# Loads on two rings in turn, alpha ahead of its unit, and a bf16 cast before the transposes, in a gated linear attention with adapters

## The chip, the cores and the metric

The kernel runs on one core of one Trainium2 chip. The metric is the device time of one execution in microseconds (us); lower is better. A core has five engines with an instruction stream each: TensorE (PE; its weight loads are shown as PEld), VectorE (DVE), ScalarE (ACT), GpSimd (POOL) and SyncE (SP). Each stream runs in order. SP and ACT can issue DMA transfers, each into a ring of its own; both rings are worked off by the same 16 DMA engines.

## What is computed

Four batches of eight heads go through a linear attention with a decay for each channel, and its output, 3072 rows of 384, through a mixture of eight low-rank adapters of which each row takes its two best:

```python
# q, k, v, alpha: (4, 8, 768, 48), f32
for t in range(S):
    state = alpha[:, :, t, :, None] * state + np.einsum('bhd,bhe->bhde', k[:, :, t], v[:, :, t])
    y[:, :, t] = np.einsum('bhd,bhde->bhe', q[:, :, t], state)
x = y.transpose(0, 2, 1, 3).reshape(B * S, H * D)      # 3072 x 384
logits = x @ w_gate                                    # 8 experts
# the two best per row, softmax over them -> w
out = x + sum(w[e] * (x @ A[e]) @ B[e] for the two e)  # A: 384 x 16, B: 16 x 384
```

## The kernel before

**Units.** The sequence is cut into chunks of 128 steps. A unit is one chunk of one batch, all eight heads: 6 chunks x 4 batches = 24 units, numbered 0 to 23. Each needs four loads of 192 KB, a chunk of alpha (a), k, q and v. In DRAM a row of a head is 48 floats, so the loads consist of pieces of 192 bytes. The loads go into two sets of buffers, one for even and one for odd batches; a load for unit u overwrites what unit u-12 read.

**Stages of a unit**, by the names that the planner uses, with the engine and the line of the operation:

- `ln` (ACT, L374): logarithm of alpha, for two units at once except for units 0 and 1.
- `cum` (PE, L379 to L385): cumulative sums of the logarithms, by matmuls with triangular matrices. `exp` (ACT, L390): their exponentials.
- `kg` (POOL, L395): k and q times these factors, to bf16. `vb` (POOL, L403): v cast to bf16.
- `tr` (PE, L409): eight transposes of kg's result. `kq` (ACT, L413): copy out of PSUM.
- `at` (PE, L421): the scores. `msk` (DVE, L426): times the causal mask.
- `st` (DVE, L433) and `kv` (PE, L441 to L446): the state from unit to unit within a batch. `av` (PE, L456 to L463): the output of the unit.
- `ysb` (ACT, L468): that output to SBUF in f32. `xt` (PE, L481): three transposes of it, in f32. `xs` (ACT, L486): copy to SBUF as bf16.
- For a group of one to three units: `z` (PE, L500) multiplies by the gate and all A; `gm`, `df`, `ge`, `gx`, `wu`, `dn`, `w` (DVE, and ACT's L524) find the two best and their weights; `zw` (DVE, L549), `zt` (PE, L558), `zs` (ACT, L564).
- For each unit `dl` (PE, L569) multiplies by B and `o` (DVE, L577) adds x. `store` (SP, L600) writes the unit's 192 KB.

**Order.** When the program is built, a list scheduler (`_order`) plays all stages with a duration for each, buffer counts (`KEEP`), PSUM slots (`SLOTS`), priorities (`PRIO`, a figure per stage, plus `PERIOD` per unit) and assumed arrival times of the loads (`_arrivals`). The order in which it starts the stages is the order in which they are emitted, and thereby the order of each engine's stream. Nothing is reordered at run time.

**Loads.** `_plan` lists them as a, k, q, v of unit 0, then of unit 1, and so on. `_ring` gives the first six to SP and ACT in turn; after them every fourth, which is v, goes to ACT and the other three to SP. On ACT a load is an entry of the planner (`ld`) and stands in ACT's stream between its activations, some 5 us (`LEAD`) before the load's assumed arrival. SP has no other work than loads and, after the last load, the stores; `pump` emits SP's loads by the planner's clock. The adapters' weights are three loads on SP (`load_weights`, L297), emitted when 20 loads are out, and three casts on DVE (`cast_weights`, L339), emitted before the first `xs`. Transfers share eight semaphores in rotation, so an issue also waits until the transfer that used its semaphore before has landed.

Of the kernel before, what the change touches and what calls it, by code (L numbers as in the profile page):

```python
# [30 lines left out]
GROUPS = [[0, 1, 2], [3, 4, 5], [6, 7, 8], [9, 10, 11], [12, 13, 14], [15, 16, 17],  # L31
          [18, 19, 20], [21, 22], [23]]
LNS = [[0], [1]] + [[u, u + 1] for u in range(2, NU, 2)]
CAST = set()
LEAD = 5.
FIRST = 6


def _ring(i, item):
    return "ACT" if (i % 2 if i < FIRST else i % 4 == 3) else "SP"  # L40

def _act(n):
# [15 lines left out]
def _pe(t):  # L62
# [3 lines left out]
SMALL = (.2, .09)  # L66
KEEP = dict(lg=2, ex=3, kg=4, kt=4, am=3, sb=2, vb=4, xs=9)
SLOTS = dict(C=1, A=1, M=3)
PRIO = dict(ln=-27.4, cum=-33.5, exp=14.2, kg=-6.0, vb=0.6, tr=4.7, kq=-8.2, at=6.7, msk=15.1,
            st=25.4, kv=6.9, av=-15.0, ysb=22.1, xb=5.9, xt=12.5, xs=-29.2, z=13.2, gm=32.7,  # L70
            df=16.8, ge=17.3, gx=21.3, wu=-9.0, dn=-22.2, w=39.9, zw=20.3, zt=1.9, zs=21.7,
            dl=6.9, o=21.2)
PERIOD = 2.0
SLACK = 0


def _plan():
    plan = []
    for u in range(NU):
        b, c = divmod(u, NCH)  # L80
        plan += [(x, b, c) for x in "akqv"]
    return plan


def _arrivals(plan):
    t, arr = 2.6, {}
    for i, (x, b, c) in enumerate(plan):
        t += 4.2 if c is None else .75
        for j in (range(NCH) if c is None else (c,)):
            arr[x, b * NCH + j] = t  # L90
        arr["due", i] = t - LEAD
    return arr


def _ops(arr):
    ops = {}

    def add(name, eng, length, deps, war=(), alloc=None, frees=None):
        ops[name] = (eng, length, list(deps), list(war), alloc, frees)

    gof = {u: g for g, us in enumerate(GROUPS) for u in us}
    lof = {u: us for us in LNS for u in us}
    prev = []
    for i, (x, b, c) in enumerate(_plan()):
        if i >= FIRST and _ring(i, (x, b, c)) == "ACT":
            war = []
            for j in (range(NCH) if c is None else (c,)):
                u = (b - 2) * NCH + j
                if u >= 0:
                    war.append(dict(a=("ln", lof[u][0]), k=("kg", u), q=("kg", u), v=("vb", u))[x])  # L110
            add(("ld", i), "ACT", (.5, .45), [("due", i)], war + prev)
            prev = [("ld", i)]
    for i, us in enumerate(LNS):
        war = [("cum", u) for u in LNS[i - KEEP["lg"]]] if i >= KEEP["lg"] else []
        add(("ln", us[0]), "ACT", _act(DM * len(us) + 30), [("a", u) for u in us], war)
    for u in range(NU):
        c = u % NCH
        p = u - KEEP["ex"]
        add(("cum", u), "PE", _pe(.49), [("ln", lof[u][0])], alloc="C")
        add(("exp", u), "ACT", _act(776), [("cum", u)],  # L120
            [("kg", p)] + ([("st", p)] if p % NCH else []), frees=("cum", u))
        p = u - KEEP["kg"]
        add(("kg", u), "POOL", _gp(768), [("exp", u), ("k", u), ("q", u)],
            [("tr", p)] + ([("kv", p)] if p % NCH < NCH - 1 else []))
        add(("vb", u), "POOL", _gpc(DM), [("v", u)], [("av", u - KEEP["vb"])])
        add(("tr", u), "PE", _pe(.48), [("kg", u)], alloc="M")
        add(("kq", u), "ACT", _act(512), [("tr", u)], [("av", u - KEEP["kt"])], frees=("tr", u))
        add(("at", u), "PE", _pe(.40), [("kq", u)], alloc="A")
        add(("msk", u), "DVE", _dve(1024), [("at", u)], [("av", u - KEEP["am"])], frees=("at", u))
        if c:  # L130
            add(("st", u), "DVE", _dve(DM), [("kv", u - 1), ("exp", u)], [("av", u - KEEP["sb"])])
        if c < NCH - 1:
            add(("kv", u), "PE", _pe(.33 if c else .17),
                [("vb", u), ("kg", u)] + ([("st", u)] if c else []),
                [] if c or not u else [("st", u - 1)])
        add(("av", u), "PE", _pe(.49 if c else .32),
            [("msk", u), ("vb", u), ("kq", u)] + ([("st", u)] if c else []), alloc="M")
        add(("ysb", u), "ACT", _act(DM), [("av", u)], frees=("av", u))
        if u in CAST:
            add(("xb", u), "POOL", _gpc(DM), [("ysb", u)])  # L140
            add(("xt", u), "PE", _pe(.17), [("xb", u)], alloc="M")
        else:
            add(("xt", u), "PE", _pe(.38), [("ysb", u)], alloc="M")
        p = u - KEEP["xs"]
        add(("xs", u), "ACT", _act(DM), [("xt", u)], [("z", gof[p])] if p >= 0 else [],
            frees=("xt", u))
    for g, us in enumerate(GROUPS):
        n = len(us)
        add(("z", g), "PE", _pe(.18 * n), [("xs", u) for u in us], alloc="M")
        add(("gm", g), "DVE", (.17 + .13 * (n - 1), .13 * n), [("z", g)])  # L150
        add(("df", g), "DVE", SMALL, [("gm", g)])
        add(("ge", g), "DVE", SMALL, [("gm", g)])
        add(("gx", g), "ACT", _act(E * n), [("df", g)])
        add(("wu", g), "DVE", SMALL, [("gx", g), ("ge", g)])
        add(("dn", g), "DVE", SMALL, [("wu", g)])
        add(("w", g), "DVE", (.4, .29), [("dn", g)])
        add(("zw", g), "DVE", _dve(P * n), [("w", g)], frees=("z", g))
        add(("zt", g), "PE", _pe(.057 * n), [("zw", g)], alloc="M")
        add(("zs", g), "ACT", _act(64 * n), [("zt", g)], frees=("zt", g))
        for u in us:  # L160
            add(("dl", u), "PE", _pe(.165), [("zs", g)], alloc="M")
            add(("o", u), "DVE", _dve(DM), [("dl", u)], frees=("dl", u))
    return ops
# [76 lines left out]
def kernel(  # L240
# [21 lines left out]
    ats = ctx.enter_context(tc.tile_pool(name="ats", bufs=KEEP["am"]))  # L262
    sbs = ctx.enter_context(tc.tile_pool(name="sbs", bufs=KEEP["sb"]))
    xss = ctx.enter_context(tc.tile_pool(name="xss", bufs=KEEP["xs"]))
    gate = ctx.enter_context(tc.tile_pool(name="gate", bufs=2))
    ps = ctx.enter_context(tc.tile_pool(name="ps", bufs=1, space=bass.MemoryType.PSUM))

# [13 lines left out]
    def view(t):  # L281
        return t.rearrange("p (h c) d -> p c h d", h=H)[:, :, :, 0:D]

    def load(item, eng):
        x, b, c = item
        t, src = home(x, b), SRC[x][b]
        if c is None:
            eng.dma_start(out=t[:, :, 0:D], in_=src.rearrange("h (c j) d -> j (h c) d", j=C))
        else:
            eng.dma_start(out=view(t)[:, c],  # L290
                          in_=src[:, c * C:(c + 1) * C, :].rearrange("h j d -> j h d"))

    W_st = consts.tile([P, E, NF, R], F4, name="W_st")
    G_st = consts.tile([P, NF, E], F4, name="G_st")
    B_st = consts.tile([P, DM], F4, name="B_st")

    def load_weights():  # L297
        nc.sync.dma_start(out=W_st.rearrange("p e i r -> p e (i r)"),  # L298
                          in_=moe_A.rearrange("e (p i) r -> p e (i r)", i=NF))
        nc.sync.dma_start(out=G_st, in_=moe_w_gate.rearrange("(p i) e -> p i e", i=NF))  # L300
        nc.sync.dma_start(out=B_st, in_=moe_B.rearrange("e r f -> (e r) f"))

    queue = list(enumerate(plan))
    for i in range(FIRST):
        load(queue.pop(0)[1], nc.sync if _ring(i, plan[i]) == "SP" else nc.scalar)
    rings = {r: [x for x in queue if _ring(*x) == r] for r in ("SP", "ACT")}

    suf = consts.tile([P, P], F2, name="suf")
    nc.gpsimd.memset(suf, 1.0)
# [260 lines left out]
                         start=True, stop=True)  # L570

    def ld(i):
        assert rings["ACT"][0][0] == i
        load(rings["ACT"].pop(0)[1], nc.scalar)

    def o(u):
        nc.vector.tensor_tensor(out=o_t[u], in0=bank("dl", u)[:, 0:DM], in1=o_t[u], op=ALU.add)  # L577
# [3 lines left out]
               w=w, zw=zw, zt=zt, zs=zs, dl=dl, o=o)  # L581
    READ = dict(a="ln", k="kg", q="kg", v="vb")
    reads = defaultdict(set)
    weights = 20
    done = []

    def pump(now):
        q = rings["SP"]
        while q:
            i, (x, b, c) = q[0]  # L590
            if arr["due", i] > now or any(
                    (b - 2) * NCH + j not in reads[x]
                    for j in (range(NCH) if c is None else (c,)) if b > 1):
                return
            load(q.pop(0)[1], nc.sync)

    def store(u):
        b, c = divmod(u, NCH)
# [2 lines left out]

    with tc.manual_schedule():
        for s, i in order:
            if (s, i) == ("xs", 0):
                cast_weights()
            RUN[s](i)
            for x, r in READ.items():
                if r == s:
                    for u in (LNS[lof[i][0]] if s == "ln" else (i,)):
                        reads[x].add(u)  # L610
            pump(when[s, i][0])
            if weights and len(plan) - len(rings["SP"]) - len(rings["ACT"]) >= weights:
                load_weights()
                weights = None
            if s == "o":
                done.append(i)
            if not rings["SP"] and not rings["ACT"]:
                while done:
                    store(done.pop(0))

# [29 lines left out]
```

## Time and profile before

| | us |
|---|---|
| median of 3 runs | 113.31 (113.3 to 113.52) |
| the profiled execution | 113.9 |
| its span, first to last instruction | 112.2 |

| engine | busy us | share of the span |
|---|---|---|
| PE | 80.6 | 72% |
| DVE | 69.1 | 62% |
| ACT | 66.2 | 59% |
| POOL | 56.2 | 50% |

The span is what the profile's rows cover; some time of an execution lies outside it. Busy time of PE is modelled at its ends, so a busy PE need not be PE at its peak. The page also has HBM reads of 19.28 MB and writes of 4.72 MB, and per line the operations that this text needs: L395 (kg) takes 1818 ns, L403 (vb) 509, L426 (msk) 1221, L390 (exp) 822, L413 (kq) 584, L468 (ysb) 483, L486 (xs) 480, and L481 (the f32 transposes) 315 a piece against 238 for the bf16 ones of L409. Landing of a load takes 4.0 to 4.5 us from its issue at the median.

How to read the views: the chain of waits follows the work that ended last back to what released it, so its shares say what the end of the execution hung on. The view of waits sums, for each operation, the time its engine stood idle before it, by what ended the wait. The windows cut the span into stretches and give busy time, the granted clock of PE (1.00 is full) and the rate of the DMA engines in each. SPq and ACTq are the issues of DMAs by SP and ACT.

### The profile page before, as it was taken

How to read it: one execution, taken by the hardware profiler on the slowest of the kernel's cores; microseconds unless marked ns; L12 is line 12 of the kernel's file. 1: busy time of each engine (PE TensorE's matmuls, PEld its weight loads, DVE VectorE, ACT ScalarE, POOL GpSimd, SP SyncE). 2: the span in 40 equal slices, each digit the busy share in tenths (PEclk: the TensorE clock that was granted, in tenths of full speed). 3: DMA queues.
4: the chain of work that ended last, by engine and by line, in shares of the span. 5: the costliest groups of instructions: out<-in, count | busy, mean ns of one | idle time of the engine just before them, and what ended most of it. 6: DMA issues, size and time to landing. Idle time of an engine off the chain costs nothing.

```text
span 112.2 us, 2916 instructions
## 1 busy us (share of the span) xinstructions
PE 80.6 (72%) x1112; PEld 62.2 (55%) x1112; DVE 69.1 (62%) x170; ACT 66.2 (59%) x128; POOL 56.2 (50%) x58
## 2 busy tenths in 40 slices
PE   0346994099995496978947969899395699996540
PEld 0124863067874286856836748579283478974210
DVE  4004330765595287899575396967289265998990
ACT  4244476046973767967818769696592745754310
POOL 5077418605949278492691676839287076000000
PEclk9999999558999999999997699999999656999975
DMA  2999999899999899999989999999899999013064
GB/s 57 259 259 259 259 230 275 181 224 212 247 240 185 165 256 237 220 244 205 230 173 214 256 241 187 246 243 229 175 259 191 338 394 390 9 72 141 3 235 186
DMA packets 104638, 24.19 MB, mean 216 GB/s; under 512 B 101424, under 2 KB 104624, under 8 KB 104624
## 3 DMA queue, kind: packets, MB, share of 16 engines
q1 hardware_dynamic: 77584, 18.89, 74.4%
q10 hardware_dynamic: 27040, 5.11, 22.7%
q8 instruction: 8, 0.13, 0.5%
q14 instruction: 6, 0.05, 0.2%
HBM read 19.28 MB, written 4.72 MB: 214 GB/s over the span
## 4 chain that ended last, share of the span: by engine, by line
SPq 39%; DMA 18%; PE 16%; DVE 16%; issue 4%; ACT 3%; DVEq 1%; POOL 1%; ACTq 0%; POOLq 0%
SPq L290 37%; DMA a_t<-in_alpha_dram 18%; DVE am L426 5%; DVE o_t L577 3%; ACT lg L374 3%; PE M_t L409 2%; PE cum_t L379 2%; DVE zw L549 2%; PE M_t L481 2%; DVE w L542 2%; PE at_t L421 2%; PE cum_t L380 1%; PE M_t L456 1%; SPq L300 1%; SPq L298 1%
## 5 line engine op out<-in xcount | busy, mean ns | idle before, releaser
L395 POOL TENSOR_TENSOR kgq<-kq_t,ex 128x768 bf16<-128x768 f32 x24 | 43.6, 1818 | 29.4 <-ACT ex L390 29.4
L426 DVE TENSOR_TENSOR am<-at_t,mask 128x1024 bf16<-128x1024 f32 x24 | 29.3, 1221 | 8.9 <-PE at_t L421 8.8
L390 ACT ACTIVATE ex<-cum_t 128x776 f32<-128x776 f32 x24 | 19.7, 822 | 5.8 <-PE cum_t L385 5.4
L379 PE MATMUL cum_t<-lg,suf 128*128 128x384 bf16 x24 | 9.0, 377 | 16.1 <-ACT lg L374 15.8
L374 ACT ACTIVATE lg<-a_t 128x768 bf16<-128x768 f32 (+1 forms) x13 | 10.3, 795 | 15.9 <-DMA a_t<-in_alpha_dram 15.9
L433 DVE TENSOR_TENSOR sb<-S_t,ex 128x384 bf16<-128x384 f32 x20 | 11.0, 551 | 13.1 <-PE S_t L446 8.7
L409 PE MATMUL M_t<-ident,kgq 128*128 128x128 bf16 x192 | 16.9, 238 | 2.7 <-POOL kgq L395 2.2
L413 ACT COPY kqt<-M_t 128x512 f32<-128x512 f32 x24 | 14.0, 584 | 8.0 <-PE M_t L409 7.7
L403 POOL CAST vb<-v_t 128x384 bf16<-128x384 f32 x24 | 12.0, 509 | 8.7 <-PE M_t L463 5.9
L409 PEld LDWEIGHTS <-kgq 128*128 128x128 bf16 x192 | 12.8, 107 | 4.9 <-POOL kgq L395 3.1
L577 DVE TENSOR_TENSOR o_t<-M_t,o_t 128x384 f32<-128x384 f32 x24 | 12.5, 551 | 3.6 <-PE M_t L569 3.4
L481 PE MATMUL M_t<-ident,o_t 128*128 128x128 f32 x72 | 14.1, 315 | 0.4 <-ACT o_t L468 0.4
L486 ACT CAST xs<-M_t 128x384 bf16<-128x384 f32 x24 | 11.2, 480 | 3.5 <-PE M_t L481 2.6
L468 ACT COPY o_t<-M_t 128x384 f32<-128x384 f32 x24 | 11.6, 483 | 1.9 <-PE M_t L463 1.9
L380 PEld LDWEIGHTS <-nsuf 128*128 128x128 bf16 x24 | 2.5, 105 | 15.5 <-issue 15.3
L481 PEld LDWEIGHTS M_t<-ident,o_t 128*128 128x128 f32 x72 | 10.2, 203 | 1.1 <-ACT o_t L468 0.9
L421 PE MATMUL at_t<-kqt 48*128 48x128 bf16 x192 | 10.6, 236 | 0.4 <-ACT kqt L413 0.4
L463 PE MATMUL M_t<-vb,am 128*128 128x48 bf16 x192 | 9.3, 189 | 0.3 <-DVE am L426 0.3
L446 PEld LDWEIGHTS <-kgq 128*128 128x128 bf16 x80 | 6.4, 110 | 5.2 <-issue 4.3
L380 PE MATMUL cum_t<-lg,nsuf 128*128 128x384 bf16 x24 | 9.2, 384 | 0.0
L441 PE MATMUL S_t<-sb,ident 128*128 128x384 bf16 x16 | 5.9, 370 | 3.5 <-DVE sb L433 3.5
L569 PE MATMUL M_t<-B_all,zs 128*128 128x384 bf16 x24 | 7.1, 338 | 1.3 <-DVE o_t L577 0.5
(47 smaller groups left out, 102.1 us busy)
## 6 DMA issues: line engine op xcount, KB each, us to landing
a_t<-in_alpha_dram SPq DMA_DIRECT2D x24, 192.0 KB, 4.3
kq_t<-in_q_dram SPq DMA_DIRECT2D x24, 192.0 KB, 4.4
v_t<-in_v_dram ACTq DMA_DIRECT2D x24, 192.0 KB, 4.0
out_dram<-o_t SPq DMA_DIRECT2D x24, 192.0 KB, 2.5
kq_t<-in_k_dram SPq DMA_DIRECT2D x22, 192.0 KB, 4.5
kq_t<-in_k_dram ACTq DMA_DIRECT2D x2, 192.0 KB, 4.3
W_st<-in_moe_A_dram SPq DMA_DIRECT2D x1, 192.0 KB, 4.6
B_st<-in_moe_B_dram SPq DMA_DIRECT2D x1, 192.0 KB, 4.0
```

Source lines behind the costliest of these rows:

```text
L290: eng.dma_start(out=view(t)[:, c], in_=src[:, c * C:(c + 1) * C, :].rearrange("h j d -> j h d"))
L374: nc.scalar.activation(lgs[i % KEEP["lg"]][:, 0:n, :, 0:D], view(a_t[b % 2])[:, c:c + n], AF.Ln)
L380: nc.tensor.matmul(cum_t[:, N0:D0], nsuf[:, :], t[:, :, 0:D], start=True, stop=True)
L390: nc.scalar.activation(st["ex"][u], cum_t[:, U0:D0 + 2 * NP], AF.Exp)
L395: nc.gpsimd.tensor_tensor(out=kgq[u % KEEP["kg"]][:, :, :, 0:D], in0=src, in1=st["ex"][u][:, 0:2 * DM].rearrange("p (w h d) -> p w h d", w ...
L403: nc.gpsimd.tensor_copy(out=st["vb"][u], in_=view(v_t[b % 2])[:, c])
L409: nc.tensor.transpose(t[:, w, p, :], pair(kgq[u % KEEP["kg"]][:, w], p), ident[:, :])
L413: nc.scalar.copy(t, bank("tr", u)[:, :])
L421: nc.tensor.matmul(at_t[:, hh, p, :], kq[rows, 0, p, :], kq[rows, 1, p, :], start=True, stop=True)
L426: nc.vector.tensor_tensor(out=st["am"][u].rearrange("p a b t -> p (a b) t"), in0=at_t.rearrange("p a b t -> p (a b) t"), in1=_bc_mid(mask[ ...
L481: nc.tensor.transpose(t[:, i * P:(i + 1) * P], x[:, i, :], idn[:, :])
L577: nc.vector.tensor_tensor(out=o_t[u], in0=bank("dl", u)[:, 0:DM], in1=o_t[u], op=ALU.add)
```

## The change

- **Rings.** `_ring(i)` now gives the loads to SP and ACT strictly in turn. ACT has 50 of them, 46 inside its stream; before it had 26, 23 inside. Eight instead of six are issued at the start.
- **Plan.** Alpha of units u+2 and u+3 is listed right behind k and q of an even unit u, ahead of v of u and of the loads of u+1. The list ends with the k and q of unit 23 and the v of units 22 and 23.
- **Weights.** They are entries of the same list, behind the loads of unit 3, in four pieces (A in halves), on the two rings in turn. The casts are emitted before the first `z` instead of the first `xs`; in DVE's stream that is behind the fourth `msk` instead of the second.
- **SP's loads** are emitted with the ACT load before them in the list, as far as the buffers' readers have been emitted, no longer by the planner's clock (`pump` is gone).
- **Cast.** `CAST` holds all units: POOL casts the unit's output to bf16 (`xb`, a 128x384 copy, into a new pool of three buffers), and the three transposes read that and write bf16 into PSUM.
- **Planner.** Other priorities and period, and slightly other durations of PE's stages and of an `ld`. This reorders the streams of all engines.

```diff
-CAST = set()
+CAST = set(range(NU))
 LEAD = 5.
-FIRST = 6
-def _ring(i, item):
-    return "ACT" if (i % 2 if i < FIRST else i % 4 == 3) else "SP"
+FIRST = 8
+def _ring(i):
+    return "ACT" if i % 2 else "SP"
...
-PRIO = dict(ln=-27.4, cum=-33.5, exp=14.2, kg=-6.0, vb=0.6, tr=4.7, kq=-8.2, at=6.7, msk=15.1,
+PRIO = dict(ln=-77.0, cum=-35.1, exp=27.5, kg=-23.8, vb=-7.9, tr=-3.7, kq=18.0, at=-4.6, msk=55.7,
...
-PERIOD = 2.0
+PERIOD = 2.3
...
 def _plan():
-    plan = []
-    for u in range(NU):
-        b, c = divmod(u, NCH)
-        plan += [(x, b, c) for x in "akqv"]
-    return plan
+    plan = [("a", 0), ("k", 0), ("q", 0), ("a", 1), ("v", 0), ("k", 1), ("q", 1), ("a", 2), ("a", 3), ("v", 1)]
+    for u in range(2, NU):
+        plan += [("k", u), ("q", u)]
+        if u % 2 == 0 and u + 2 < NU:
+            plan += [("a", u + 2), ("a", u + 3)]
+        if u < NU - 2:
+            plan += [("v", u)]
+        if u == 3:
+            plan += [("w", 0), ("w", 1), ("w", 2), ("w", 3)]
+    return plan + [("v", NU - 2), ("v", NU - 1)]
...
-            add(("ld", i), "ACT", (.5, .45), [("due", i)], war + prev)
+            add(("ld", i), "ACT", (.4, .1), [("due", i)], war + prev)
...
+    xbs = ctx.enter_context(tc.tile_pool(name="xbs", bufs=3))
...
     def ld(i):
-        assert rings["ACT"][0][0] == i
-        load(rings["ACT"].pop(0)[1], nc.scalar)
+        assert loaded <= i
+        while loaded <= i or (loaded < len(plan) and _ring(loaded) == "SP" and free(loaded)):
+            load_next()
+
+    def free(i):
+        x, u = plan[i]
+        return u < 2 * NCH or u - 2 * NCH in reads[x]
...
-            if (s, i) == ("xs", 0):
+            if (s, i) == ("z", 0):
                 cast_weights()
             RUN[s](i)
...
-            pump(when[s, i][0])
-            if weights and len(plan) - len(rings["SP"]) - len(rings["ACT"]) >= weights:
-                load_weights()
-                weights = None
```

The functions that the cast brings into use stand in the kernel before too, where no unit was in `CAST`:

```python
    def xb(u):
        st["xb"][u] = xbs.tile([P, DM], F2, name="xb")
        nc.gpsimd.tensor_copy(out=st["xb"][u], in_=o_t[u])

    def xt(u):
        if u in CAST:
            t, x, idn = bank("xt", u).bitcast(F2), st["xb"][u], ident
        else:
            t, x, idn = bank("xt", u), o_t[u], ident4
```

## The prediction

> **What bounds the kernel now.** I read the chain of waits first, then the waits, then the span by stages with the DMA queues beside them, and last the timeline of the two queues that issue loads. The chain that ended last runs mostly through load issues on SP and landings of alpha:
>
> ```profile
> SPq 39%; DMA 18%; PE 16%; DVE 16%; issue 4%; ACT 3%; DVEq 1%; POOL 1%; ACTq 0%; POOLq 0%
> SPq L290 37%; DMA a_t<-in_alpha_dram 18%; DVE am L426 5%; DVE o_t L577 3%; ACT lg L374 3%; PE M_t L409 2%; PE cum_t L379 2%; DVE zw L549 2%; PE M_t L481 2%; DVE w L542 2%; PE at_t L421 2%; PE cum_t L380 1%; PE M_t L456 1%; SPq L300 1%; SPq L298 1%
> ```
>
> SP's issue of loads (L290) and the flight of alpha make 55% of the span; no engine has more than 16%. The waits say who stands still for it (total, times, longest, in us):
>
> ```profile
> POOL kgq L395 <- ACT ex L390: 29.4, 18, 4.9
> ACT lg L374 <- DMA a_t<-in_alpha_dram: 15.9, 10, 2.7
> DVE W L340 <- DMA W_st<-in_moe_A_dram: 4.4, 1, 4.4
> ```
>
> The logarithm waits for alpha, and POOL's product waits for the exp behind it: one wait, seen twice. DVE stands 4.4 us for the weights early on. Next the stages (us; busy time and instructions of PE, PEld, DVE, ACT, POOL; clock, DMA share, GB/s):
>
> ```profile
> 4.00:13.00 9.00, 5.55 (x54) 4.09 (x54) 1.78 (x2) 3.73 (x6) 4.96 (x5) 1.00 1.28 259
> 35.50:38.00 2.50, 0.33 (x6) 0.22 (x5) 1.02 (x2) 0.92 (x2) 1.59 (x2) 1.00 0.83 166
> 40.00:50.00 10.00, 8.43 (x143) 7.01 (x140) 8.39 (x17) 7.81 (x16) 7.57 (x6) 1.00 1.19 238
> 57.00:60.00 3.00, 0.73 (x13) 0.51 (x12) 1.33 (x2) 1.24 (x4) 1.74 (x2) 1.00 0.85 160
> 88.00:96.00 8.00, 7.99 (x91) 6.40 (x91) 4.49 (x12) 4.26 (x9) 4.09 (x3) 0.60 0.99 366
> 96.00:112.20 16.20, 9.54 (x115) 6.22 (x112) 12.55 (x43) 5.92 (x17) 0.00 (x0) 0.87 0.30 110
> ```
>
> Loads move at 259 GB/s in some stages and at 160 to 166 in others, and in the slow ones PE all but stops. The queues of 4 to 13 us and, below the dots, of 57 to 60 us tell the two apart (packets, MB, share; q1 is SP's ring, q10 ACT's):
>
> ```profile
> q1 hardware_dynamic: 7139, 1.35, 73.9%
> q10 hardware_dynamic: 5188, 0.98, 53.7%
> ...
> q1 hardware_dynamic: 2492, 0.47, 83.6%
> q10 hardware_dynamic: 50, 0.01, 1.6%
> ```
>
> With both rings filled, 259; with SP's alone, 160. (From 71 to 74 us SP's ring alone did reach 233, so this is not a law.) ACT's ring runs dry where ACT stands at a logarithm whose alpha is not there, with the next v load queued behind it. The timeline shows what an issue costs (start, us):
>
> ```profile
> 2.07 1.20 ACTq L290 DMA_DIRECT2D kq_t<-in_k_dram  x1
> 5.74 1.46 SPq L290 DMA_DIRECT2D kq_t<-in_k_dram  x1
> 43.83 0.84 ACT L374 ACTIVATE lg<-a_t 128x768 bf16<-128x768 f32 x1 [0.81 <-DMA a_t<-in_alpha_dram]
> 43.86 0.40 ACTq L290 DMA_DIRECT2D v_t<-in_v_dram  x1
> ```
>
> Into a full ring an issue takes 1.20 to 1.46 us; into an empty one 0.40, and then it lies wholly under an ACTIVATE that is running.
>
> **Alternating rings and alpha ahead.** The page has 19.28 MB read; they flow from 2 us to about 88.5 us (after that the windows carry stores at 395 GB/s): 19.28/86.5 = 223 GB/s. If all were two states of 259 and 163, the one-ring state held (259-223)/96 = 37% of the time. Bounds: 259 throughout ends the loads at 2+74.4 = 76.4 us; nothing gained leaves 88.5. The slow stages I checked end with an alpha landing, which is the wait that alpha two units earlier takes away, and ACT has every second load now. I keep a third of the one-ring time for other stalls of ACT, 12.5%: 259-12 = 247 GB/s, 78.1 us, last load at T = 80.1.
>
> The Trainium skill speaks against this term: "DMA: Bandwidth & Descriptors", section "Issuing engines are not separate DMA queues", says that DMAs from several engines share the same 16 DMA engines and that spreading them saves only the issue time. By that rule the rate would stay at 223 and this term would be nothing. The rows above (259 against 160) differ from it.
>
> **What follows the last load.** Now alpha of unit 23 lands near 87.1 and the span ends at 112.2, 25 us later. In the new order k and q of unit 23 land two loads (2 x 0.76 us at 259 GB/s) before T. Then come the product of unit 22, still in front (1.82), its own (1.82), transposes (0.61), kqt copy (0.58), scores (0.40), mask (1.22), and some 0.1 us for each of four hand-overs: 6.85. The last mask ends at T-1.5+6.85 = T+5.3. From the last mask (100.0 + 1.2) to the end of the span the trace has 11.0 us. The cast adds 0.50 (the vb cast is the same shape: median 0.503) and a hand-over of 0.1, the bf16 transposes take off 0.2: 11.4.
>
> **Transposes and cast.** Six f32 transposes in a row took 0.92 us at full clock, eight bf16 ones 0.61, one alone 0.28 and 0.22 (medians): pitch (0.92-0.28)/5 = 0.128 against (0.61-0.22)/7 = 0.056, so 3 x 0.07 = 0.21 us of PE per unit, 5 us in all. On the path I take none but the last: PE waits for loads. POOL gets 24 x 0.50 = 12.1 us, 56.2 -> 68.3; it now idles 29.4 for exp, which hides it. Per unit POOL has 1.82+2x0.50 = 2.83 us against four loads in 3.18 us (786 KB at 247 GB/s): 89% busy. Without that cover the whole 12 us is on the path. What is queued behind a cast that waits for ysb is the product of a later unit, and PE's transposes wait for that.
>
> **Issues on ACT.** ACT issues 50 loads, 46 within its stream, against 26 and 23. 23 more x 0.38 = 8.7 us; under running ACTIVATEs they cost nothing (44 us row), else 8.7, and at 1.46 each far more (rival three). Queued behind each is ACT's exp or one of its copies out of PSUM, for which PE waits. Every load also waits for the landing eight loads earlier, 8 x 0.76 = 6.1 us against a median of 4.0 to 4.5: nothing.
>
> **Weights.** The casts now come behind the fourth mask instead of the second, and the weights are items 19 to 22 of the plan, landed near 18 to 20 us. The fourth mask ends near 3.9 + 16 x 0.755 + 5 = 21 us (first landing 3.9, q of unit 3 the 17th load), so the 4.4 us wait goes. The new priorities reorder all four streams. The nearest rows are the waits that the order itself makes, DVE's mask for the scores (8.8 us in all) and ACT's kqt copy for the transposes (7.7): the new order could take most of 8 away or add as much. I take +1.8, half a unit's pace now (3.6), as nothing shows a better order. Stores still queue on SP behind the last load, 15 at 0.5 us each as now, under the tail: nothing. Loads into reused buffers wait for readers twelve units back: nothing, as now (under 8 us of SP's time, spread, with a full ring behind it).
>
> **Sum.** 80.1 + 5.3 + 11.4 = 96.8. As a check by units: 4 masks by 21 us, 20 more at 3.18 = 84.6, + 11.4 = 96.0. Do the engines keep up? From 40 to 50 us loads came at 238 GB/s, 3.30 us per unit, and DVE's 8.39 us at 2.77 per unit ((69.1-2.6)/24) are 3.03 units, so they followed at exactly that pace with PE and DVE at 84%. With the 1.8 for the new order the span is 98.6. The profiled execution took 113.9 for a span of 112.2 (1.7 outside), and the median is 113.31, 0.6 less: 98.6 + 1.7 - 0.6 = **99.7 us**.
>
> **Rivals.** One: the rings share one limit and the rate stays at 223; only the shorter tail is won. 88.5+5.3+11.4+1.8+1.1 = 108.1. For it: 233 on SP's ring alone at 71 us; against: 259 wherever both are filled. Two: the engines become the bound. POOL, at 2.83 us, DVE at 2.77 and ACT at 2.70 per unit are within 5% of each other, POOL's casts stand in front of products, and a pace of 3.6, as the loads have it now, gives 21+72+11.4+1.1 = 105.5. For it: no stage yet ran faster than 3.3 for long; against: those stages were short of loads. Three, slower: the full ring moves from SP, which has nothing else to do, to ACT, and each blocked issue holds back exp and the copies behind it. At pace p the time is 33.5+20p; it passes 113.5 at p = 4.0, that is 1.3 us per unit over ACT's 2.70, or 0.68 us uncovered for each of its 1.92 issues. SP's rows (0.95 median for k, 1.46 in a full ring) less 0.38 reach that: at 0.8 p = 4.24, 118 us. Against it: ACT's ring is full only when ACT is ahead of the loads, and then its time is cheap.
>
> **Chances.** Forecast 58%, own range 95 to 104. Two 13%, one 13%, three 14%, little change 2%. A measurement of this kernel tells 0.2% from no change; faster 84%, within 0.2% 2%, slower 14%. Below, 259 GB/s throughout and no lag give 76.4+5.3+11.4+1.1 = 94.2; above, case one with 3 us of worse order is 111, and most of case three is left out: 94 to 111.
>
> **What would show it.** Right: few windows under 200 GB/s before 80 us; q10 near half of the load packets; ACT's wait for alpha under 5 us; stores starting near 78; the cast of W without a wait; six transposes at L482 near 0.5 us. Wrong: both rings filled at 220 (one); POOL over 90% busy mid-span and PE waiting for the product (two); ACTq issues over 0.8 us with PE waiting for ACT's copies (three).

## The result, and the profile after

| | before | after |
|---|---|---|
| median of 4 runs, us | 113.31 (112.75 to 113.52) | 118.61 (118.39 to 118.89) |
| span of the profiled execution, us | 112.2 | 117.0 |

The changed kernel is slower: ratio 1.0477, 95% interval 1.0433 to 1.0522. The forecast was 99.7. Ratios, here and below, compare fast executions alone (within 1.5% of the fastest of the same kernel) while medians are over all, so a ratio can differ from the quotient of two medians.

From the page of the changed kernel, first the rate of the DMA engines in 40 slices of 2.9 us, then the two rings of loads (q1 is SP's, q10 ACT's), then the chain that ended last:

```profile
GB/s 52 259 259 251 220 187 259 278 192 224 236 255 258 188 249 257 257 257 257 229 220 262 213 219 353 198 303 211 108 246 247 178 261 15 0 67 134 22 206 178
...
q1 hardware_dynamic: 54048, 14.27, 51.9%
q10 hardware_dynamic: 50592, 9.74, 41.4%
...
SPq 23%; DVE 22%; DMA 20%; PE 18%; issue 5%; ACT 5%; ACTq 2%; DVEq 1%; POOL 0%
```

Both rings carry loads, and most slices before 60 us stand at 220 to 259 GB/s. The rate that the forecast counted on is there in that time, and yet the end is late. The windows of the changed kernel show where (busy us and instructions of PE, PEld, DVE, ACT, POOL; clock, DMA share, GB/s):

```profile
30.00:40.00 10.00, 7.02 (x82) 5.50 (x81) 6.81 (x16) 4.64 (x8) 6.17 (x6) 1.00 1.22 246
40.00:50.00 10.00, 6.67 (x92) 4.81 (x92) 5.00 (x7) 5.95 (x11) 5.46 (x6) 0.83 1.18 240
50.00:60.00 10.00, 7.99 (x102) 6.22 (x99) 5.57 (x15) 5.13 (x11) 5.91 (x7) 0.66 1.20 239
70.00:80.00 10.00, 8.54 (x148) 6.53 (x142) 9.46 (x20) 8.33 (x17) 8.81 (x10) 1.00 1.07 281
```

From 40 to 50 us the kernel before had 238 GB/s and 8.39 us of DVE, 7.81 of ACT; the changed one has 240 GB/s and 5.00 and 5.95. Bytes arrive as fast as they did, and the engines do less with them: these are not the bytes that the next unit needs. By the starts of the exps in the timeline, the first twelve units take 4.6 us each (6.52 to 56.73 in eleven steps), the last twelve 3.1 each (61.46 to 95.66), which is the pace of the forecast (3.18). The clock, at 0.83 and 0.66 in two of these windows, does not explain the loss: the changed kernel's four executions had mean granted clocks of 0.92, 0.91, 0.87 and 0.85 and took 118.72, 118.39, 118.89 and 118.5 us.

The waits of the changed kernel (total, times, longest, us):

```profile
POOL xb L473 <- ACT o_t L469: 22.3, 15, 3.4
POOL kgq L396 <- ACT ex L391: 10.7, 3, 5.1
ACT lg L375 <- DMA v_t<-in_v_dram: 3.9, 2, 3.2
ACT lg L375 <- DMA a_t<-in_alpha_dram: 2.9, 1, 2.9
ACT ex L391 <- DMA a_t<-in_alpha_dram: 2.5, 1, 2.5
ACT o_t L469 <- DMA kq_t<-in_k_dram: 2.5, 1, 2.5
ACT zs L565 <- DMA kq_t<-in_k_dram: 2.1, 1, 2.1
ACT xs L487 <- DMA v_t<-in_v_dram: 1.2, 1, 1.2
```

Of these ACT rows only the logarithm's wait for alpha is a wait for its own data. The logarithm reads no v, the exp no alpha in SBUF, and the copies L469, L565 and L487 read PSUM alone. What stood still was a load in front of them in ACT's stream. The timeline of the changed kernel shows one such place (start, us; in brackets the idle time before):

```profile
19.75 0.83 ACT L375 ACTIVATE lg<-a_t 128x768 bf16<-128x768 f32 x1
20.62 1.20 SPq L303 DMA_DIRECT2D v_t<-in_v_dram  x1
...
22.64 0.37 ACTq L303 DMA_DIRECT2D kq_t<-in_q_dram  x1
23.05 0.48 ACT L469 COPY o_t<-M_t 128x384 f32<-128x384 f32 x1 [2.46 <-DMA kq_t<-in_k_dram]
...
23.59 0.51 POOL L473 CAST xb<-o_t 128x384 bf16<-128x384 f32 x1 [3.39 <-ACT o_t L469]
...
24.06 1.81 POOL L396 TENSOR_TENSOR kgq<-kq_t,ex 128x768 bf16<-128x768 f32 x1
```

ACT is free at 20.58. Its next instruction is the load of q, and it is issued only at 22.64. That is no slow issue (it takes 0.37 us): the load signals its landing through a semaphore that both rings share, eight of them in all, and is not issued before the semaphore's previous user has landed (in all traces of this case no issue comes earlier than 0.016 us after that landing). That user was a load of SP's, landed at 22.61: the k of unit 6, item 31 of the list, while the load that stands for it is the q of unit 4, item 24. Behind the load stands the copy out of PSUM, behind the copy POOL's cast waits 3.39 us, and behind the cast stands the product (24.06), whose exp had ended at 19.86.

By the trace, 47 of ACT's loads take a semaphore that was used before, and 22 of them are issued within 0.06 us of the landing of its previous user, 18 times a transfer of SP's; in the kernel before it is 3 of 23. In front of 16 of the 22 ACT's engine was idle, for 15.8 us in all (1.0 us in the kernel before); the others lay under an operation that was still running. Of the 22 previous users, 13 are loads that stand later in the list, up to 31 places, and 3 are stores. SP meanwhile, which has nothing else to do, runs ahead (timeline, SP's last two loads and its first store, then ACT's last load):

```profile
64.02 0.37 SPq L303 DMA_DIRECT2D kq_t<-in_k_dram  x1
64.44 1.26 SPq L303 DMA_DIRECT2D v_t<-in_v_dram  x1
65.81 1.52 SPq L595 DMA_DIRECT2D out_dram<-o_t  x1
...
93.74 0.37 ACTq L303 DMA_DIRECT2D v_t<-in_v_dram  x1
```

SP has issued its loads for units 22 and 23 when ACT has just started the exp of unit 13 (63.33). ACT's last load of the same units comes 29 us later.

### The profile page after: what moved, and what is told of

It reads as the page before. It is cut to its first block, busy times and chain, and to the rows that moved or that the text cites. A ratio compares the mean times of both kernels' runs of the same rounds, so it can differ in the third digit from the quotient of the medians.

```text
span 117.0 us, 2963 instructions
## 1 busy us (share of the span) xinstructions
PE 81.7 (70%) x1112; PEld 59.9 (51%) x1112; DVE 71.7 (61%) x170; ACT 65.9 (56%) x128; POOL 67.2 (57%) x82
## 3 DMA queue, kind: packets, MB, share of 16 engines
HBM read 19.28 MB, written 4.72 MB: 205 GB/s over the span
## 4 chain that ended last, share of the span: by engine, by line
SPq 23%; DVE 22%; DMA 20%; PE 18%; issue 5%; ACT 5%; ACTq 2%; DVEq 1%; POOL 0%
SPq L303 21%; DMA kq_t<-in_k_dram 9%; DMA v_t<-in_v_dram 7%; DVE am L427 7%; DMA a_t<-in_alpha_dram 4%; DVE o_t L583 4%; PE M_t L570 4%; PE M_t L410 3%; DVE w L543 3%; DVE zw L550 2%; SPq L300 2%; ACTq L303 2%; PE M_t L501 2%; PE at_t L422 2%; DVE sb L434 2%
## 5 line engine op out<-in xcount | busy, mean ns | idle before, releaser
L473 POOL CAST xb<-o_t 128x384 bf16<-128x384 f32 x24 | 12.2, 508 | 27.8 <-ACT o_t L469 22.3
L410 PE MATMUL M_t<-ident,kgq 128*128 128x128 bf16 x192 | 17.9, 248 | 1.8 <-POOL kgq L396 1.5
L380 PE MATMUL cum_t<-lg,suf 128*128 128x384 bf16 x24 | 9.8, 408 | 11.0 <-ACT lg L375 10.3
L410 PEld LDWEIGHTS <-kgq 128*128 128x128 bf16 x192 | 14.2, 113 | 4.1 <-POOL kgq L396 3.1
L469 ACT COPY o_t<-M_t 128x384 f32<-128x384 f32 x24 | 11.5, 481 | 7.9 <-PE M_t L464 4.5
L487 ACT COPY xs<-M_t 128x384 bf16<-128x384 bf16 x24 | 11.2, 486 | 6.9 <-DMA a_t<-in_alpha_dram 1.6
L570 PE MATMUL M_t<-B_all,zs 128*128 128x384 bf16 x24 | 8.5, 391 | 3.9 <-ACT zs L565 2.2
L482 PE MATMUL M_t<-ident,xb 128*128 128x128 bf16 x72 | 8.6, 238 | 2.0 <-ACT xs L487 1.4
L501 PE MATMUL M_t<-W,xs 128*128 128x136 bf16 x72 | 6.7, 238 | 4.4 <-ACT xs L487 1.8
L422 PEld LDWEIGHTS <-kqt 48*128 48x128 bf16 x192 | 6.4, 104 | 6.6 <-ACT kqt L414 4.8
L457 PE MATMUL M_t<-sb,kqt 128*128 128x96 bf16 x80 | 7.3, 218 | 1.9 <-ACT xs L487 0.8
```

Of the source, the lines that this page charges most:

```text
L410: nc.tensor.transpose(t[:, w, p, :], pair(kgq[u % KEEP["kg"]][:, w], p), ident[:, :])
L422: nc.tensor.matmul(at_t[:, hh, p, :], kq[rows, 0, p, :], kq[rows, 1, p, :], start=True, stop=True)
L473: nc.gpsimd.tensor_copy(out=st["xb"][u], in_=o_t[u])
L570: nc.tensor.matmul(bank("dl", u)[:, 0:DM], st["zs"][g][:, j * P:(j + 1) * P], B_all[:, :], start=True, stop=True)
```

## The experiments

The theory in all expectations is that ACT's loads stand for SP's; the rivals change. Each run has its own runs of the kernel before on the same chip, so ratios are to be compared, not times. Unless said otherwise the edit is made in the changed kernel and its compute streams stay as they are.

**One ring, the cast, and later issues.** Three edits and the combination of the first two:

```diff
# e1_sp_only
-        eng = nc.sync if _ring(loaded) == "SP" else nc.scalar
+        eng = nc.sync if loaded >= FIRST or _ring(loaded) == "SP" else nc.scalar
# e2_no_cast (e3_sp_only_no_cast has both)
-        nc.gpsimd.tensor_copy(out=st["xb"][u], in_=o_t[u])
-            t, x, idn = bank("xt", u).bitcast(F2), st["xb"][u], ident
+            t, x, idn = bank("xt", u), o_t[u], ident4
# e4_late3
+            if s == "ld":
+                late.append([i, 3])   # issued behind three more of ACT's computing instructions
```

> All loads behind the first eight are issued by SP, in the order of the plan; every other instruction of ACT, PE, DVE and POOL stays as in the changed kernel. Theory A (ACT stands at its own loads until an earlier transfer's semaphore comes free, 20 us by the waits of ACT ended by a DMA, and exp and the copies out of PSUM queue behind it): 100 to 108 us; only waits for alpha are left of ACT's waits for DMAs, and the floor is the rate of one ring. Theory B (the cast before the products in POOL's stream costs the time): 115 or more.

> Rings, plan and streams as in the changed kernel, but no cast on POOL, and f32 transposes of the f32 output as before. Theory A: 115 to 119 us, ACT's waits for DMAs still near 20 us. Theory B: 105 to 110, and POOL's products start without the 22 us that the cast waited for ACT's copy.

> Both edits: all loads on SP and no cast. Theory A: within 2 us of the run with all loads on SP alone. Theory B: within 2 us of the run without the cast alone. If the two work in a row (ACT's stall delays the copy, the copy delays the cast, the cast the next product), it is lower than each of them.

> The changed kernel with each of ACT's loads three of ACT's compute instructions later in its stream (never behind a reader of it); rings, plan, cast and the order of all compute unchanged. Theory A: ACT's waits ended by a DMA fall to under 10 us and the time to 106 to 114, though the loads themselves go out later. Theory B: within 1 us of 118.6.

| run | median, us | before | ratio |
|---|---|---|---|
| e1_sp_only | 116.53 | 111.88 | 1.0401 (1.0228 to 1.0574) |
| e2_no_cast | 121.35 | 111.88 | 1.0917 (1.0822 to 1.1011) |
| e3_sp_only_no_cast | 116.18 | 111.88 | 1.0348 (1.0121 to 1.0574) |
| e4_late3 | 119.23 | 111.88 | 1.0697 (1.0547 to 1.0847) |

None is faster than the kernel before. The cast is not what makes the changed kernel slow: without it the kernel is slower still. The expectations of theory A missed for three of the four (only the two runs with SP alone lie within 2 us of each other), and theory B fell with the run without the cast. With SP alone, ACT stands no more at loads, but the kernel is short of bytes (the GB/s row of its page, then its waits):

```profile
GB/s 51 259 259 232 219 229 136 213 219 215 223 165 208 227 165 197 211 206 165 197 198 217 191 157 209 207 185 188 211 215 175 194 213 246 346 391 390 66 207 176
```

```profile
ACT lg L375 <- DMA a_t<-in_alpha_dram: 13.6, 9, 2.9
POOL kgq L396 <- DMA kq_t<-in_q_dram: 10.2, 11, 2.4
POOL vb L404 <- DMA v_t<-in_v_dram: 8.9, 8, 2.3
```

The last load lands at 99.4 us: 19.28 MB / (99.4 - 2) = 198 GB/s. All three waits are now waits for data. So this edit takes one cause away and puts another in its place, and its total cannot price the first. Its first half says more: the first twelve units take 3.3 us each (6.47 to 42.89), against 4.6 in the changed kernel, though the loads came at 194 GB/s from 30 to 60 us against 241. In the changed kernel the first half lacks order, not rate. Issuing ACT's loads later fails in another way: what ACT doesn't wait at the issue, the readers wait for the data (logarithm for alpha 6.9 us, vb for v 5.3, kg for q 4.4), and ACT's waits ended by a DMA fall only from 20.5 us to 15.5, where under 10 was expected. The theory, that the place of the loads in ACT's stream is the fault, falls in this form. Three instructions later, 19 loads are still issued within 0.06 us of the landing they stand for. That made the next theory: the fault is that SP runs ahead.

**How far ahead SP may run.** Chunk buffers for six or four units instead of twelve hold SP back by itself, as it may not overwrite what isn't read:

```diff
+KS = 4                                  # f6_slots: 6
-    a_t = [big.tile([P, H * NCH, HP], F4, name=f"a_t{i}") for i in range(2)]
+    a_t = big.tile([P, H * KS, HP], F4, name="a_t")
...
     def free(i):
-        return u < 2 * NCH or u - 2 * NCH in reads[x]
+        return u < KS or u - KS in reads[x]
```

> The changed kernel with buffers for 6 units instead of 12, so that a load for unit u waits for the readers of unit u-6; the order of all streams stays. Theory A2 (SP, which waits for nothing else, runs up to 11 units ahead of need and fills the DMA engines and the shared semaphores with loads that nobody waits for, while each of ACT's loads, every second one needed, waits for a semaphore of SP's and comes late): SP can be 5 units ahead at most, so the loads on ACT get more of the first 60 us; 108 to 115 us, first twelve units under 4.3 us each against 4.6. Rival (the order of the streams, PE, DVE and POOL, sets the pace of the first half): no change, 118 to 119, or slower from the added waits for buffers.

> As the run with 6 units, with 4. Theory A2: SP is held to three units ahead, 102 to 112 us, first twelve units at 3.3 to 4.0 us each, unless the waits for buffers now cost SP's ring its fill (then the rate falls under 230 GB/s). Rival: 118 or more.

| units of buffers | ratio | of 47 ACT loads, issued within 0.06 us of that landing | ACT idle in front of these, us | SP's largest lead, units | SP's last load, us |
|---|---|---|---|---|---|
| 12 (the changed kernel) | 1.0477 (1.0433 to 1.0522) | 22 | 15.8 | 11 | 64.4 |
| 6 | 1.018 (1.006 to 1.0301) | 15 | 13.9 | 5 | 75.4 |
| 4 | 0.9988 (0.9923 to 1.0053) | 13 | 8.2 | 3 | 76.1 |

The lead is the unit of a k or q load less the number of POOL's products started at its issue; ACT's own such loads are one or two units ahead in all three. The medians are 114.27 for six (before 113.12) and 112.65 for four (ten runs), the second a little over its range. Fewer buffers, less time, and in step with it a smaller lead of SP and less standing of ACT. The first twelve exps take 4.0 us each with six units (6.37 to 49.99) and 3.4 with four (6.48 to 44.29), both as expected. At the end something new stands out (timeline of the run with four units):

```profile
76.71 6.58 SPq L595 DMA_DIRECT2D out_dram<-o_t  x8
...
77.50 0.60 ACT L414 COPY kqt<-M_t 128x512 f32<-128x512 f32 x1
...
81.67 0.42 ACTq L303 DMA_DIRECT2D kq_t<-in_q_dram  x1
82.13 0.84 ACT L375 ACTIVATE lg<-a_t 128x768 bf16<-128x768 f32 x1 [4.03 <-DMA v_t<-in_v_dram]
```

SP, done with its loads, issues eight stores. ACT has three of its loads still to come, and its load of q stands from 78.1 to 81.67 for the landing of SP's v at 81.64; the next one waits for a store's landing (issued at 83.92, the store landed at 83.85). The last logarithm, of units 22 and 23, comes behind the first of these, 4.9 us after its alpha landed (77.2).

**The parts alone, in the kernel before.** Here the planner makes a new order around the edit.

```diff
# p1_alternate
-    return "ACT" if (i % 2 if i < FIRST else i % 4 == 3) else "SP"
+    return "ACT" if i % 2 else "SP"
# p3_cast
-CAST = set()
+CAST = set(range(NU))
```

> The kernel before with one edit: loads strictly in turn on both rings (k and v on ACT), its own plan, no cast. Theory A2: slower than before by 3 to 8 us, with ACT standing at its loads. Rival (the alternation by itself helps, the new order or plan is what costs): 102 to 110 us.

> The kernel before with one edit: the cast on POOL and bf16 transposes; rings and plan as before. Expected within 2 us of before, as PE is short of loads and POOL idles; faster by 1 to 3 us if the 5 us of PE time lie on the path in the stages in which loads come fast.

Strict alternation alone: 127.71 us, ratio 1.1325 (1.1165 to 1.1484), the largest loss of the study and, at 14.6 us, far over the 3 to 8 that the theory gave. The cast alone: 116.96, ratio 1.0389 (1.0266 to 1.0512), 3.8 us where under 2 was expected; the new order that the planner makes around it is in that price. The waits of the first show the changed kernel's mark again, an exp behind a load and a product behind the exp:

```profile
POOL kgq L395 <- ACT ex L390: 37.7, 18, 6.9
...
ACT ex L390 <- DMA a_t<-in_alpha_dram: 7.5, 3, 3.5
```

**The end, and three to one.** In the runs named f4 the buffers hold four units, in f12 twelve. "As before" in the first expectation means as in the run with four units above, not as in the kernel before.

```diff
# f4_tail (f4_tail_no_cast: the cast is also left out, as in e2_no_cast)
-        eng = nc.sync if _ring(loaded) == "SP" else nc.scalar
+        eng = nc.sync if _ring(loaded) == "SP" or loaded >= len(plan) - 10 else nc.scalar
# f4_three_to_one
+        act = loaded % 2 if loaded < FIRST else loaded % 4 == 3 and loaded < len(plan) - 10
+        eng = nc.scalar if act else nc.sync
# f12_three_to_one (twelve units, as changed)
+        eng = nc.scalar if (loaded % 2 if loaded < FIRST else loaded % 4 == 3) else nc.sync
```

> The changed kernel with chunk buffers for four units, as before, and in addition its last ten loads (units 21 to 23 and v of unit 20) all on SP, so that none of ACT's loads stands in its stream behind a store; the compute streams are those of the changed kernel. Theory (ACT's in-stream loads stand for semaphores that SP's transfers hold, in the first stage SP's early loads, at the end SP's stores): with four units ln(22,23) ran at 82.1 us because ACT stood at its q load until 81.67; alpha of unit 23 landed at 77.2 there, so ln(22,23) comes at 77.5 to 79 and the end, 28 us later, makes a span of 105 to 107, a time of 107 to 110. Rival (the tail is bound by the products and copies, whatever ACT's last loads do): span 109 to 111, time 111.5 to 113.5, as with four units alone.

> As the run with the last ten loads on SP, but behind the first eight ACT carries each fourth load only instead of each second; SP has the rest; the compute streams are the same. Theory (each load in ACT's stream may stand for a semaphore, so fewer are better; SP is never far ahead with four units of buffers, so little stands there): the same time as its sister run within 1.5 us, one ring more lightly and one more heavily loaded, rate 230 to 255 GB/s over the first 60 us. Rival (strict alternation itself is what gives the rate): rate near the 200 to 223 GB/s of one ring or of the kernel before, the last load some 8 us later, time 113 to 118.

> The changed kernel with its buffers for twelve units, where behind the first eight loads ACT carries each fourth load and SP the rest; the compute streams are the changed kernel's. Theory (the harm is ACT's loads standing for SP's semaphores while SP runs ahead): half as many loads on ACT, SP's still ahead of need, so part of the loss goes: ACT's waits ended by DMA fall from some 20 us to 8 to 14, time 113 to 116.5. Rival (the new order of the compute streams is what costs, whatever the rings do): 117.5 to 119.5. Rival (the share of the rings alone decides, three to one being right): under 112.

> As the run with four units of buffers and the last ten loads on SP, but without GpSimd's cast: the attention output is transposed in f32 as in the kernel before; nothing else changes. The cast's price where loads come in time. Theory (GpSimd's 24 casts stand before its kg products and wait for ACT's copies, but six f32 transposes of a unit cost PE more): without it 1 to 4 us slower than its sister run, as it was with twelve units (121.35 against 118.61). Rival (the cast in front of kg is on the path once loads are not): 1 to 4 us faster.

| run | median, us | before | ratio |
|---|---|---|---|
| f4_tail | 108.08 | 112.82 | 0.947 (0.9359 to 0.9581) |
| f4_three_to_one | 111.81 | 112.82 | 0.9785 (0.9657 to 0.9912) |
| f12_three_to_one | 110.04 | 112.82 | 0.9721 (0.9626 to 0.9817) |
| f4_tail_no_cast | 106.07 (104.3 to 110.29) | 112.82 | not settled by four runs, see below |

With the last ten loads on SP the time came as expected (span 107.1, at the upper end of 105 to 107), but not by the way expected: the logarithm of units 22 and 23 came at 81.49 (79.79 when the kernel was run again, see below), hardly before the 82.13 of the run with four units, as the alpha of unit 23, now ACT's last load, landed only at 80.02. From there to the end it took 25.6 us instead of 28.0. That part fits the theory, as ACT has no load left behind that logarithm, where in the other run two more stood 0.58 and 0.92 us; the rest of the 2.4 us is not traced. With three to one and twelve units, all of the loss goes, more than the 113 to 116.5 that the theory had given. Its trace tells why: SP, with three quarters of the bytes, now issues its last load at 85.46 us, beside ACT's last at 85.56. It has no time to run ahead (its lead is 2 units at most), and 6 of ACT's 24 loads stand at a landing, with ACT idle for 5.2 us in front of them. By the number alone, the rival that three to one is simply the right share had it (under 112). The sister runs with four units speak against it: where SP is held back by buffers, alternating is the better (108.08 against 111.81), since three to one costs rate. The windows from 30 to 60 us, first of three to one, then of alternating, both with four units:

```profile
30.00:60.00 30.00, 23.17 (x355) 17.48 (x355) 19.99 (x41) 20.62 (x40) 21.27 (x24) 0.91 1.03 206
```

```profile
30.00:60.00 30.00, 26.01 (x413) 19.83 (x411) 23.86 (x49) 24.44 (x47) 24.95 (x28) 0.94 1.18 236
```

So the expectation of "the same time within 1.5 us" for that pair missed, and its rival, that alternation gives the rate, was right: 206 against 236 GB/s, and the last load 8.3 us later (94.19 against 85.85), though the time stayed under its 113 to 118. The kernel before, by the same window, had 215.

**The two open points.** Is most of the loss made at the end, and which sign has the cast's price?

```diff
# f12_tail: the edit of f4_tail in the changed kernel, with its twelve units
+        eng = nc.sync if _ring(loaded) == "SP" or loaded >= len(plan) - 10 else nc.scalar
```

> The changed kernel with its buffers for twelve units, and only its last ten loads all on SP. Theory (most of the loss is made in the first twelve units, 4.6 us each against 3.1 behind them, where ACT's loads stand for SP's transfers): the end is mended and the first half is not, time 114.5 to 118; the first twelve units again 4.3 to 4.8 us each. Rival (most of it is made at the end, where ACT's last loads stand behind SP's stores): 107 to 112, near the 108.1 of the same edit with four units of buffers.

> The kernel of the run with four units of buffers and the last ten loads on SP, once more, in the same rounds as its sister run without the cast. 107 to 109.5 by either theory.

> The kernel of the run with four units of buffers, the last ten loads on SP and f32 transposes without the cast, once more, in the same rounds as its sister run with the cast. Theory (where loads come in time the cast costs: it stands before kg on GpSimd and waits there for ACT's copy): 1 to 3 us below the sister run. Rival (the first difference was the chips' spread): within 0.7 us of it, or above it.

The end mended alone gives 120.85 us, ratio 1.0899 (1.0811 to 1.0986): no gain, and nearly 3 us above the range of the theory; where these 3 us come from stays open. The first twelve units take 4.5 us each (6.56 to 56.22), as the theory had it. So most of the loss is not made at the end. The windows of this run in its first half are much like those of the changed kernel (clock 0.67 and 0.69 against 0.83 and 0.66):

```profile
40.00:50.00 10.00, 8.11 (x97) 6.00 (x97) 5.33 (x8) 5.12 (x9) 5.83 (x7) 0.67 1.25 252
50.00:60.00 10.00, 7.65 (x96) 5.77 (x95) 6.25 (x15) 4.77 (x9) 5.54 (x7) 0.69 1.21 242
```

Four units, the last ten loads on SP, with the cast: 106.94 us, ratio 0.965 (0.96 to 0.9701). The same without the cast: **104.11 us, ratio 0.9301 (0.9189 to 0.9413)**, the fastest kernel of the study; both beside 111.39 of the kernel before. By the medians the cast costs 2.8 us here, by the ratios 3.5% of the kernel before. The last expectation had it so; the one for the first pair had expected the opposite sign, so the rival named there was right. The waits of the version with the cast show it:

```profile
POOL xb L473 <- ACT o_t L469: 16.2, 15, 2.9
POOL kgq L396 <- ACT ex L391: 8.9, 3, 5.1
```

The casts stand before the products and wait 16.2 us for ACT's copies. Without them the first row is gone, POOL's wait for exps is 11.6 us (12.9 in the second run), and from 40 to 70 us the engines keep the pace of the loads (windows of the first run without the cast):

```profile
40.00:50.00 10.00, 9.30 (x146) 7.28 (x147) 8.01 (x19) 8.26 (x16) 7.28 (x6) 1.00 1.25 254
50.00:60.00 10.00, 9.75 (x158) 8.02 (x157) 8.98 (x19) 9.12 (x19) 8.00 (x8) 1.00 1.27 258
60.00:70.00 10.00, 8.49 (x139) 6.80 (x136) 7.74 (x19) 7.71 (x16) 7.40 (x8) 1.00 1.25 252
```

Here PE is at 85 to 98% and the loads at 252 to 258 GB/s, a little more than the 84% and 247 GB/s that the prediction had counted on for the changed kernel.

## Why the prediction was wrong

**The step that failed** is in the part on issues on ACT: "Every load also waits for the landing eight loads earlier, 8 x 0.76 = 6.1 us against a median of 4.0 to 4.5: nothing." It took the eight semaphores as if the loads used them in the order of the list, evenly, from one place. They are issued by two streams, one of which is free and the other busy, and the program does not hand the semaphores out in the order of the list: ACT's q of unit 4 stands for SP's k of unit 6, its v of unit 11 for SP's q of unit 19. SP's loads run up to 11 units ahead of need; ACT's load, which is needed within one or two units, waits for a semaphore that a fresh transfer of SP's holds. The wait was priced at nothing; in the changed kernel 22 of 47 ACT loads show it, ACT is idle for 15.8 us in front of 16 of them, and everything behind them in ACT's stream waits along. Holding SP back by buffers (1.048, 1.018, 0.999) or by giving it more to carry (0.972) shrinks the loss or takes it away with the same compute streams (what semaphore a load gets changes with these edits too); mending the end, moving ACT's loads three instructions down or leaving out the cast does not (1.090, 1.070, 1.092). ACT's loads are not longer in flight for SP's early bytes: 3.8 to 4.3 us from issue to landing at the median, against 4.0 to 4.3 in the kernel before and 4.2 to 4.8 with four units. They come late because they are issued late. How much of the loss is ACT's standing itself and how much the lateness of the data that it brings isn't separated by these runs.

**In the sum**, the span of 98.6 became 117.0. The last load landed at 97.56 instead of T = 80.1, which is 17.5 of the 18.4 us. The last mask ended 6.6 us after it instead of 5.3, the tail took 12.8 instead of 11.4, and against these stands the 1.8 that the sum held for a worse order, which the runs do not show by itself: 17.5 + 1.3 + 1.4 - 1.8 = 18.4.

**The rate** was right as long as both rings had loads: 246, 240 and 239 GB/s from 30 to 60 us against 247. Over the whole load it was 19.28 MB in 95.6 us, 202 GB/s. T followed from it only if the bytes came in the order of need. SP's half was issued by 64.4 us and ACT's other half at the speed of ACT's own stream. The rule of the Trainium skill that was weighed against this term ("DMA: Bandwidth & Descriptors", section "Issuing engines are not separate DMA queues": another issuing engine saves only issue time) differs from the runs here: from 30 to 60 us the loads came at 194 GB/s with SP's ring alone, at 206 with three to one and at 236 with alternation.

**Rival three** had the place right and the number (118, for 0.8 us uncovered at each load), the number by luck: ACT is held at its loads and exps and copies stand behind it. Its mechanism was another. It looked for issues of over 0.8 us into a full ring; only 5 of ACT's 50 took that long, most 0.37 to 0.6. The wait stands before the issue, where the profile books it to the next computing instruction.

**The cast** was costed at nothing, hidden under POOL's wait for exps. The sentence on what is queued behind it (the product of a later unit) named the danger and gave it no price. Where loads come in time it costs 2.8 us by the medians, and 3.9% in the kernel before, there with a new order of the streams. With twelve units it was the other way round (1.092 without it, 1.048 with it); why is not settled.

**Right:** alpha two units ahead takes ACT's wait for it from 15.9 us to 2.9, the bf16 transposes and the later casts of W hold nothing up for long (DVE's wait for W_st is gone), and the pace of 3.18 us per unit is there (3.1) as soon as SP has run out of loads. With SP held back, the loads at the end on SP and no cast, T was 81.8 us and the span 102.6 in the first run of it, against 80.1 and 98.6.

## What to carry to other kernels

When loads are split between a queue whose engine does nothing else and one whose engine computes, ask how far the free one can run ahead: if only the buffers limit it, more buffers can make a kernel slower, and an even split was a loss here until they were cut. A wait that ends with a transfer the instruction doesn't read is the mark of a load in front of it that stands for another load. Price a shared resource (here eight semaphores) by who holds it at the moment of need, not by its count times the mean pace.

## What was not expected of the hardware

One ring did not fill the DMA engines with these pieces of 192 bytes: 198 GB/s over the whole load with SP's alone, 259 in stretches with both filled. PE's granted clock also fell without a gap of over 1.4 us: in windows of 1 us of the changed kernel it is 1.00 until 50 us and 0.50 from 51 to 57, behind a stretch (47 to 50 us) in which PE was busy for 0.97 of 3 us; the waits in front of its matmuls were 1.4 us and shorter, and at 0.50 PE was then busy without a break from 52 to 57. In the fastest kernel's first run the clock stayed at 1.00 from 30 to 90 us.
